# Two FFN layers behind pooled attention: the second layer's table ring in two pools, its first two units interleaved, other store queues

## Chip, cores and metric

The kernel runs on one core of one Trainium2 chip, as one program. The metric is the time of one execution in microseconds on the device; times before are the median of three runs.

## What is computed

The reference, cut to what matters:

```python
# pooled attention: q, k, v are [8, 8, 576, 64]; keys and values are means of 8 positions
k_p = k.reshape(B, H, S // 8, 8, D).mean(axis=3)
v_p = v.reshape(B, H, S // 8, 8, D).mean(axis=3)
x = softmax(scale * q @ k_p.T) @ v_p          # as [4608, 512]
# layer 1: w_in [512, 2048], w_out [2048, 512]
h = x @ w_in
x = (h * clip(h + 3, 0, 6) / 6) @ w_out
# layer 2: w_gate, w_val [512, 1536], w_out [1536, 512]
g = x @ w_gate
out = (g / (1 + exp(-g)) * (x @ w_val)) @ w_out
```

## The kernel before

Every matmul operand in fp32 is split into a rounded part ("hi") and the remainder ("lo"), and a product is hi·hi + hi·lo + lo·hi: three matmuls. Layer 1's down step and all of layer 2 use a seven-product scheme for a 2x2 block product (Strassen in Winograd's form): the quarters 11, 12, 21, 22 of the left operand and sums S1 to S4 of them, those of the right operand and sums T1 to T4, products P1 to P7. The weight side of these sums (the *tables*) is made beside layer 1 and stored in DRAM (`sw1`, `sup`, `sdn`).

The tokens go through layer 1 in nine blocks of 512 (`j`), the up step of all blocks first, then the down step block by block, product by product (`down_b`, `split_b`, `evac_b`; the loop `for i in range(7 * NB)`, n = i mod 7). Its results y go to DRAM by the stores of `evac_b`; in the last block the stores of the products n = 5 and 6 are kept in `last_y` and issued behind the loop, on SyncE's queue, like all the others.

Layer 2 goes through six groups (`p`) of 768 tokens. A group is an up stage of 12 *units* (f, m), where m = 0 is the gate and m = 1 the value table of hidden pair f, and then a down stage of seven products (`down2`, `evac`). A unit is seven products of six matmuls (128x384), each product in a PSUM bank of its own, in the order of the list `UP`: P1 (operand 11), P6 (T2), P5 (T1), P2 (21), P4 (T4), P7 (T3), P3 (22). ScalarE copies P1 out of its bank, VectorE adds the others to that copy (the tiles `c`).

The right operands `xc` of group p + 1 are made from the y of that group (`ystg`) by `x_step` in seven steps: ScalarE casts the hi part, VectorE subtracts for the lo part, and VectorE makes the next sum in place in `ystg`. For group 0 the steps stand at the end of layer 1's last block: step 0 at n = 5, steps 1 to 3 at n = 6, the rest behind the loop. The operand of the last step, T3, is in the pool `xt`, which lies over layer 1's result tiles.

Tables come through a ring of four tiles (`ring`, 8 KB a partition each). A unit takes two: products of the table places 0 to 3 in the first (1024 KB), places 4 to 6 in the second (768 KB). `load_next` issues the next unit's two loads on SyncE's queue. For group 0 it is called at n = 5 and n = 6 of layer 1's last block, then after each unit. The ring's memory is that of layer 1's first weight (`px`) and of operands of its down step (`gq`).

The order on each engine is that of the code (a manual schedule): an instruction that waits holds up all that stands behind it on its engine or queue. Waits between engines are put in from tile uses; with `reuse_waits="tile"` a new tile waits for the last users of the memory it lies over.

Of the kernel before, what the change touches and what calls it, by code (L numbers as in the profile page):

```python
# [23 lines left out]
def kernel(  # L24
# [27 lines left out]
    nc = tc.nc  # L52
# [26 lines left out]
    prep_ctx = ExitStack()  # L79
    s7_p = ctx.enter_context(tc.tile_pool(name="s7", bufs=1, side="right"))  # L80
    q7_p = ctx.enter_context(tc.tile_pool(name="q7", bufs=1, side="right"))
    stg_p = prep_ctx.enter_context(tc.tile_pool(name="stg", bufs=3, side="right"))
# [582 lines left out]
    def x_step(p, n, lo_eng, sum_eng):  # L665
# [10 lines left out]
        xc[p, what] = x  # L676
        split(x[:, 0], x[:, 1], v(what), lo_eng)
        if then:
            sums_b(sum_eng, v, (then,))

    def ring_tile():
        return l2["ring"].tile([P, 2048], F32R, tag="wr", name="wr")
# [65 lines left out]

    TURN = {"11": "11", "22": "22", "21": "12", "12": "21"}
# [28 lines left out]
    def down2(p, n):  # L778
        what = DN[n][0]
        b = dn_b[what] = [bank()[:, :2 * P] for i in range(PT)]  # L780
        for c in range(NPAIR // CH):
            g = gc.pop((p, n, c))
            for t in range(PT):
# [7 lines left out]
    def evac(p, n):  # L791
# [40 lines left out]
        else:  # L832
            add(o_t["o12"], o_t["o12"])
            store("o12", 0, 1)

# [5 lines left out]
    lb, last_y = {}, []  # L841
# [9 lines left out]
    def new_pw(n, t):  # L851
        lb["pw", DN[n][2]] = t.rearrange("p (f a n) -> p f a n", f=NP1, a=2)

    def load_pw(n, half):
        what, fs = DN[n][2], slice(NP1 // 2 * half, NP1 // 2 * (half + 1))
        nc.sync.dma_start(
            out=f32(lb["pw", what][:, fs]).rearrange("p f a n -> p (f a n)"),
# [19 lines left out]
    def down_b(i):  # L877
# [7 lines left out]
        for c in range(NCB):  # L885
            g = gb.pop((i, c))
            for d in range(2):
                for k in range(CB):
                    for m, (wh, gh) in enumerate(((0, 0), (0, 1), (1, 0))):
                        nc.tensor.matmul(  # L890
                            out=ps[:, d], lhsT=w[:, CB * c + k, wh, P * d:P * (d + 1)], rhs=g[:, gh, k],
# [4 lines left out]
    def evac_b(j, n):  # L896
# [11 lines left out]
        def store(tag):  # L908
            r, c = int(tag[1]) - 1, int(tag[2]) - 1
            t0 = N * j + MB * r  # L910
            send = lambda t=ob[tag]: nc.sync.dma_start(out=y_d[:, 2 * c:2 * c + 2, t0:t0 + MB], in_=t)
            if last and n >= 5:
                last_y.append(send)
            else:
                send()
# [227 lines left out]
    with tc.manual_schedule():  # L1143
# [64 lines left out]
        for j in range(NB):  # L1208
            for f in range(F1):
                if (j, f) == (NB - 1, 0):  # L1210
                    attn_ctx.close()
                    for nm in ("px", "gq"):
                        lb[nm] = right_b.enter_context(
# [61 lines left out]
        for send in last_y:  # L1275
            send()
# [64 lines left out]
```

## Time and profile before

| | |
|---|---|
| timed runs, us | 1751.06 median (1749.9 to 1751.83) |
| profiled execution, us | 1746.81 |
| its span, us | 1745.0 |
| TensorE matmul busy, us | 1692.8 (97% of the span) |
| VectorE, ScalarE, GpSimd busy, us | 1334.7, 753.4, 639.0 |
| granted TensorE clock, mean | 0.988 of full speed |
| moved by DMA, MB | 432.47 |

The profiled execution is 4.25 us below the median of the timed runs; sums are made against it. Layer 1's down step ends near 943 us, layer 2 fills the rest. The granted clock has two levels, full (2.4 GHz) and half (1.2 GHz).

### The profile page before, as it was taken

What the parts mean: (1) busy time and instruction counts of PE and PEld (TensorE: products, weight loads), DVE (VectorE), ACT (ScalarE), POOL (GpSimd) and SP (SyncE); (2) the same over time, 40 slices, a digit from 0 to 9 for tenths busy, and PEclk for the clock granted to TensorE, in tenths of its full rate; (3) what the DMA queues carried; (4) which work ended last, traced back from release to release, by engine and by line L of the source; (5) the groups of instructions that cost most, each with busy time, mean ns of one, the idle gap of its engine ahead of it and who ended that gap; (6) DMA issues with size and microseconds to landing.
All of it is one profiled execution on the core that took longest, in us unless ns stands there. A gap on an engine that the chain in (4) does not pass through costs nothing.

```text
span 1745.0 us, 30719 instructions
## 1 busy us (share of the span) xinstructions
PE 1692.8 (97%) x11116; PEld 1598.5 (92%) x11116; DVE 1334.7 (76%) x2356; ACT 753.4 (43%) x1656; POOL 639.0 (37%) x821
## 2 busy tenths in 40 slices
PE   5889999999999999999998999999999999999999
PEld 4678887878788999999998999999999999999999
DVE  6888897788975678888887668668668668668666
ACT  6665555555544455555554224224224224224223
POOL 6554765756821000000000550550550560560560
PEclk8899999999999999999999999999999999999999
DMA  7766898888777965566545878878878878878776
GB/s 184 175 188 176 252 263 242 261 256 256 222 251 278 418 257 174 203 226 216 219 155 188 282 243 289 296 242 291 294 242 292 296 241 289 299 243 285 268 241 218
DMA packets 235832, 432.47 MB, mean 248 GB/s; under 512 B 86688, under 2 KB 168608, under 8 KB 218528
## 3 DMA queue, kind: packets, MB, share of 16 engines
q1 hardware_dynamic: 234624, 430.25, 74.8%
q8 instruction: 88, 1.44, 0.3%
q14 instruction: 64, 0.52, 0.1%
q10 hardware_dynamic: 1056, 0.26, 0.1%
HBM read 326.11 MB, written 104.33 MB: 247 GB/s over the span
## 4 chain that ended last, share of the span: by engine, by line
PE 79%; DVE 8%; DMA 7%; POOL 2%; ACT 2%; issue 1%; SPq 1%; DVEq 0%; POOLq 0%; ACTq 0%
PE b L711 45%; PE b L890 19%; PE h L622 12%; DMA q_in<-in_q_dram 1%; DVE g L637 1%; PE pss L502 1%; DMA qv<-in_q_dram 1%; DMA wstg<-in_moe_w_out_dram 1%; DMA gq<-g 1%; DMA y<-o 1%; DVE mx L512 1%; POOL v_in L441 1%; DMA k_in<-in_k_dram 1%; DVE s L278 1%; DVE qT L484 1%
## 5 line engine op out<-in xcount | busy, mean ns | idle before, releaser
L711 PE MATMUL b<-xc,wr 128*128 128x384 f32 x3024 | 529.1, 336 | 5.2 <-ACT xc L149 2.2
L711 PEld LDWEIGHTS b<-xc,wr 128*128 128x128 f32 x3024 | 526.4, 189 | 6.8 <-ACT xc L149 2.5
L622 PE MATMUL h<-x,wu 128*128 128x512 f32 x1728 | 428.7, 400 | 6.8 <-DVE g L637 6.8
L758 POOL TENSOR_TENSOR s<-s,c 128x384 f32<-128x384 f32 x144 | 142.5, 1014 | 752.3 <-ACT s L756 752.1
L720 DVE TENSOR_TENSOR c<-c,b 128x384 f32<-128x384 f32 x504 | 265.1, 552 | 175.6 <-PE b L711 151.8
L622 PEld LDWEIGHTS h<-x,wu 128*128 128x128 f32 x1728 | 319.3, 190 | 72.2 <-DVE g L637 8.6
L890 PEld LDWEIGHTS b<-gb,pw 128*128 128x128 f32 x3024 | 353.1, 188 | 0.6 <-DVE gb L150 0.5
L890 PE MATMUL b<-gb,pw 128*128 128x256 f32 x3024 | 353.3, 279 | 0.3 <-DVE gb L150 0.3
L711 PE MATMUL b<-wr,gc 128*128 128x256 f32 x2268 | 265.6, 279 | 0.0
L711 PEld LDWEIGHTS b<-wr,gc 128*128 128x128 f32 x2268 | 265.4, 188 | 0.0
L149 ACT CAST gb<-gq 128x512 fp32r<-128x512 f32 x252 | 155.3, 621 | 157.0 <-PE b L890 138.7
L150 DVE TENSOR_TENSOR gb<-gq,gb 128x512 fp32r<-128x512 f32 x252 | 167.4, 689 | 50.7 <-ACT gb L149 50.0
L765 POOL TENSOR_TENSOR gf<-s,c 128x384 f32<-128x384 f32 x144 | 168.2, 1192 | 67.4 <-DVE c L720 64.5
L149 ACT CAST gc<-gf 128x768 fp32r<-128x768 f32 x126 | 105.7, 839 | 187.1 <-POOL gf L765 100.9
L756 ACT ACTIVATE s<-c 128x384 f32<-128x384 f32 x144 | 73.5, 526 | 198.9 <-DVE c L720 197.8
L150 DVE TENSOR_TENSOR gc<-gf,gc 128x768 fp32r<-128x768 f32 x126 | 134.1, 1094 | 16.4 <-ACT gc L149 14.2
L633 ACT ACTIVATE g<-h,half 128x512 f32<-128x512 f32 x144 | 99.0, 687 | 69.7 <-PE h L622 57.5
L637 DVE SCALAR_TENSOR_TENSOR g<-g,h 128x512 f32<-128x512 f32 x144 | 97.4, 677 | 20.2 <-ACT g L633 19.2
L550 POOL TENSOR_TENSOR e<-e,sm 128x288 f32<-128x288 f32 (+4 forms) x74 | 48.1, 650 | 117.7 <-DVE sm L546 95.6
L728 ACT COPY c<-b 128x384 f32<-128x384 f32 x72 | 33.9, 470 | 127.9 <-PE b L711 127.9
L868 DVE TENSOR_TENSOR gq<-gq 128x1024 f32<-128x1024 f32 x72 | 87.8, 1219 | 0.0
L207 DVE TENSOR_TENSOR gf<-gf 128x768 f32<-128x768 f32 (+1 forms) x66 | 67.0, 1030 | 12.2 <-POOL gf L765 10.9
(101 smaller groups left out, 1657.5 us busy)
## 6 DMA issues: line engine op xcount, KB each, us to landing
wr<-sup SPq DMA_DIRECT2D x72, 1024.0 KB
wr<-sdn SPq DMA_DIRECT2D x84, 768.0 KB
wr<-sup SPq DMA_DIRECT2D x72, 768.0 KB
g<-g SPq DMA_DIRECT2D x144, 256.0 KB
gq<-g SPq DMA_DIRECT2D x36, 1024.0 KB
sup<-s SPq DMA_DIRECT2D x12, 1792.0 KB
wstg<-in_moe_w_out_dram SPq DMA_DIRECT2D x56, 256.0 KB
sw<-s SPq DMA_DIRECT2D x8, 1792.0 KB
```

The costliest lines, as they stand in the source:

```text
L149: nc.scalar.copy(out=hi, in_=src)
L150: lo_engine.tensor_tensor(out=lo, in0=src, in1=f32(hi), op=ALU.subtract)
L622: nc.tensor.matmul(out=ps, lhsT=w(kt, wh), rhs=x(kt, xh), start=first and n == 0, stop=last and n == 3 * len(kts) - 1,)
L633: nc.scalar.activation(out=t, in_=ps, func=ACTF.Relu, bias=half, scale=1.0 / 6.0)
L637: nc.vector.scalar_tensor_tensor(out=t, in0=t, scalar=1.0, in1=ps, op0=ALU.min, op1=ALU.mult)
L711: nc.tensor.matmul(out=ps, lhsT=w(wh), rhs=x(xh), start=first and n == 0, stop=last and n == 2)
L720: add = lambda dst, a, b: nc.vector.tensor_tensor(out=dst, in0=a, in1=b, op=ALU.add)
L756: nc.scalar.activation(out=g[q], in_=c[q], func=ACTF.Sigmoid)
L758: nc.gpsimd.tensor_tensor(out=g[q], in0=g[q], in1=c[q], op=ALU.mult)
L765: nc.gpsimd.tensor_tensor(out=gf[p][:, GP[TURN[q]], f], in0=g[q], in1=c[q], op=ALU.mult)
L868: nc.vector.tensor_tensor(out=v(what), in0=v(a), in1=v(b), op=op)
L890: nc.tensor.matmul(out=ps[:, d], lhsT=w[:, CB * c + k, wh, P * d:P * (d + 1)], rhs=g[:, gh, k], start=what == place and (c, d, k, m) == (0 ...
```

## The change

- The ring's four tiles are now two pools of two, `ra` over the memory of layer 1's first weight `pw(0)` (which is now kept in two halves, in tiles of `ra`) and `rb` over operands `gq`. Units take `ra` and `rb` in turn. The first `load_next` stands at n = 2 of layer 1's last block instead of n = 5, the second at n = 5 instead of n = 6.
- The operands T1, 22, T2 are in `xa`; T3, 21, T4 are in `xb`, now on the other side of the memory, over layer 1's weights. The steps go 11, T1, 22, T2, T3, 21, T4.
- The stores of y of the last block are issued on GpSimd's queue, each in its place; `last_y` is gone.
- The first two units of group 0 are made by `up2_pair`, product by product for both m, with P6, P7 and P4 added onto P1's bank and P3 onto P5's.
- In the last group the last down product goes bank by bank, and each third is added and stored by itself.

The core of the diff:

```diff
@@ x_step @@
-        what, then = [("11", "T1"), ("22", "T3"), ("T1", "T2"), ("T2", None), ("21", "T4"), ("T4", None), ("T3", None)][n]
+        what, then = [("11", ("T1",)), ("T1", ()), ("22", ("T3", "T2")), ("T2", ()), ("T3", ()), ("21", ("T4",)), ("T4", ())][n]
         if what == "11":
-            x = new_q7("xc")[:, :4 * M].rearrange("p (a k n) -> p a k n", a=2, k=2)
+            x = new_q7("xc")[:, :4 * M]
+        elif what in ("T1", "22", "T2"):
+            x = l2["xa"].tile([P, 4 * M], F32R, tag="x" + what, name="xc")
         else:
-            pool = l2["xa" if what in ("T1", "22") else "xt" if what == "T3" else "xb"]
-            x = pool.tile([P, 2, 2, M], F32R, tag="x" + what, name="xc")
+            x = l2["xb"].tile([P, 4 * M + 32], F32R, tag="x" + what, name="xc")[:, 8:8 + 4 * M]
...
     def ring_tile():
-        return l2["ring"].tile([P, 2048], F32R, tag="wr", name="wr")
+        n_ring[0] += 1
+        if (n_ring[0] - 1) // 2 % 2:
+            return l2["rb"].tile([P, 2048], F32R, tag="wr", name="wr")
+        return l2["ra"].tile([P, 2048 + 32], F32R, tag="wr", name="wr")[:, :2048]
...
+    def up2_pair(p, f):
+        ps, c, mul = {}, [{}, {}], nc.tensor.matmul
+        for what, wa, xb in [("P1", "11", "11"), ("P5", "S1", "T1"), ("P6", "S2", "T2"), ("P7", "S3", "T3"),
+                             ("P3", "S4", "22"), ("P2", "12", "21"), ("P4", "22", "T4")]:
+            for m in range(2):
+                place = {"P6": "P1", "P7": "P1", "P4": "P1", "P3": "P5"}.get(what, what)
+                if place == what:
+                    ps[m, what] = bank()[:, :M]
+                b, w, x = ps[m, place], wr.pop(("up", (f, m), A7[wa])), xc[p, xb]
+                for n in range(6):
+                    k, (wh, xh) = n // 3, ((0, 0), (0, 1), (1, 0))[n % 3]
+                    mul(out=b, lhsT=w[:, wh, k], rhs=x[:, xh, k], start=place == what and n == 0,
+                        stop=n == 5, skip_group_check=True)
+                new = {"P1": "11", "P6": "12", "P7": "22", "P4": "21"}.get(what)
+                if new:
+                    c[m][new] = tmp(f"c{new}{m}")
+                    nc.scalar.copy(out=c[m][new], in_=b)
+                done = {"P7": ("22", "P5"), "P3": ("12", "P5"), "P2": ("11", "P2")}.get(what)
+                if done:
+                    t = c[m][done[0]]
+                    nc.vector.tensor_tensor(out=t, in0=t, in1=ps[m, done[1]], op=ALU.add)
+        return c
...
@@ down2 @@
+        order = [(c, t) for c in range(NPAIR // CH) for t in range(PT)]
+        if (p, n) == (NG - 1, 6):
+            order.sort(key=lambda ct: ct[1])
@@ evac, last product @@
+        else:
+            o = o_t["o12"]
+            for t in range(PT):
+                nc.vector.tensor_tensor(out=o[:, t], in0=o[:, t], in1=b[t], op=ALU.add)
+                t0 = 2 * M * p + P * t
+                (nc.sync, nc.scalar, nc.sync)[t].dma_start(out=out[t0:t0 + P, 2 * P:], in_=o[:, t])
@@ evac_b @@
-            send = lambda t=ob[tag]: nc.sync.dma_start(out=y_d[:, 2 * c:2 * c + 2, t0:t0 + MB], in_=t)
-            if last and n >= 5:
-                last_y.append(send)
-            else:
-                send()
+            (nc.gpsimd if last else nc.sync).dma_start(out=y_d[:, 2 * c:2 * c + 2, t0:t0 + MB], in_=ob[tag])
@@ layer 1's down loop @@
+            if (j, n) == (NB - 1, 2):
+                load_next()
             if j == NB - 1 and n >= 5:
                 if n == 5:
                     right_b.close()
-                    prep_ctx.close()
-                    for nm, bufs in (("xa", 1), ("ring", 4), ("xb", 1)):
+                    for nm, bufs in (("xa", 1), ("rb", 2)):
...
-                load_next()
+                    load_next()
@@ layer 2 @@
-                c = up2(p, (f, m))
+                if p == f == 0:
+                    if m == 0:
+                        pair = up2_pair(p, f)
+                    c = pair[m]
+                else:
+                    c = up2(p, (f, m))
```

TensorE at the start of layer 2, before: b is the PSUM bank, xc the operand, wr the table tile (11476 and 11478 of the first unit, 11538 and 11540 of the second).

```order
L890 MATMUL b_11489<-gb_11461,pw_7267 128x256 x12
L711 MATMUL b_11587<-xc_11480,wr_11476 128x384 x6
L711 MATMUL b_11596<-xc_11550,wr_11476 128x384 x6
L711 MATMUL b_11605<-xc_11546,wr_11476 128x384 x6
L711 MATMUL b_11614<-xc_11554,wr_11476 128x384 x6
L711 MATMUL b_11622<-xc_11558,wr_11478 128x384 x6
L711 MATMUL b_11630<-xc_11572,wr_11478 128x384 x6
L711 MATMUL b_11640<-xc_11542,wr_11478 128x384 x6
L711 MATMUL b_11664<-xc_11480,wr_11538 128x384 x6
```

The same place now (tables 11271 and 11273 of the first unit, 11476 and 11478 of the second):

```order
L931 MATMUL b_11491<-gb_11466,pw_7268 128x256 x12
L764 MATMUL b_11583<-xc_11480,wr_11271 128x384 x6
L764 MATMUL b_11592<-xc_11480,wr_11476 128x384 x6
L764 MATMUL b_11601<-xc_11540,wr_11271 128x384 x6
L764 MATMUL b_11608<-xc_11540,wr_11476 128x384 x6
L764 MATMUL b_11583<-xc_11548,wr_11271 128x384 x6
L764 MATMUL b_11592<-xc_11548,wr_11476 128x384 x6
L764 MATMUL b_11583<-xc_11561,wr_11273 128x384 x6
L764 MATMUL b_11592<-xc_11561,wr_11478 128x384 x6
```

Each operand now serves two products in a row, one for each unit, and the third pair of products (P6) goes into the banks of the first (11583, 11592).

ScalarE at the same place, before: casts of the operands xc, then the copy of the first P1 (c from bank b) and the sigmoids s.

```order
L149 CAST xc<-ystg 128x768
L927 COPY o_11484<-b 128x512
L149 CAST xc<-ystg 128x768 x6
L728 COPY c_11594<-b 128x384
L756 ACT_TABLE_LOAD
L756 ACTIVATE s_11652<-c_11594 128x384
```

ScalarE now:

```order
L148 CAST xc<-ystg 128x768
L964 COPY o_11484<-b 128x512
L148 CAST xc<-ystg 128x768 x6
L769 COPY c_11590<-b 128x384
L769 COPY c_11599<-b 128x384
L769 COPY c_11621<-b 128x384
L769 COPY c_11629<-b 128x384
L769 COPY c_11637<-b 128x384
L769 COPY c_11646<-b 128x384
```

The six casts stand ahead of the first copy in both; the one copy of a unit has become four, for two units.

SyncE's queue from the load of the first group's y (`ystg`) on, before (sup_107 is the table of unit (0,0), sup_108 of (0,1), sup_109 of (1,0)):

```order
L662 DMA ystg<-y 128x2x384 x4
L690 DMA wr<-sup_107 128x2048
L690 DMA wr<-sup_107 128x1536
L690 DMA wr<-sup_108 128x2048
L690 DMA wr<-sup_108 128x1536
L911 DMA y<-o_11486 128x2x256
L911 DMA y<-o_11484 128x2x256
L911 DMA y<-o_11141 128x2x256
L690 DMA wr<-sup_109 128x2048
```

SyncE's queue now, from the loads of the first table on:

```order
L694 DMA wr<-sup_107 128x2048
L694 DMA wr<-sup_107 128x1536
L661 DMA ystg<-y 128x2x384 x4
L694 DMA wr<-sup_108 128x2048
L694 DMA wr<-sup_108 128x1536
L694 DMA wr<-sup_109 128x2048
L694 DMA wr<-sup_109 128x1536
```

The first table stands ahead of the y loads, and the y stores are gone from this queue.

## Rows read from the trace of the kernel before

**Rows 1.** The page, part 4: the chain's shares of the span by line

```profile
PE b L711 45%; PE b L890 19%; PE h L622 12%; DMA q_in<-in_q_dram 1%; DVE g L637 1%; PE pss L502 1%; DMA qv<-in_q_dram 1%; DMA wstg<-in_moe_w_out_dram 1%; DMA gq<-g 1%; DMA y<-o 1%; DVE mx L512 1%; POOL v_in L441 1%; DMA k_in<-in_k_dram 1%; DVE s L278 1%; DVE qT L484 1%
```

**Rows 2.** The chain in order of time, 900 to 1000 us: start, us, what

```profile
942.00 12.08 DMA y<-o
...
954.10 0.84 ACT xc L149
```

**Rows 3.** TensorE's timeline, 936 to 1090 us: start, us, engine, what, [idle before <-releaser]

```profile
935.77 7.04 PE L890 MATMUL b<-gb,pw 128*128 128x256 f32 x59
944.94 6.38 PE L711 MATMUL b<-xc,wr 128*128 128x384 f32 x25 [2.13 <-DMA wr<-sup]
951.68 1.14 PE L711 MATMUL b<-xc,wr 128*128 128x384 f32 x5 [0.36 <-DVE xc L150]
954.98 0.44 PE L711 MATMUL b<-xc,wr 128*128 128x384 f32 x1 [2.17 <-ACT xc L149]
955.98 83.59 PE L711 MATMUL b<-xc,wr 128*128 128x384 f32 x473 [0.55 <-DVE xc L150]
```

**Rows 4.** Windows: stretch, us, busy time of each engine, PEclk, DMA share, GB/s

```profile
945.00:948.00 3.00, 2.96 (x9) 2.45 (x10) 2.10 (x4) 1.56 (x2) 0.00 (x0) 0.53 1.04 391
...
957.00:959.00 2.00, 2.00 (x8) 2.00 (x8) 1.99 (x5) 0.95 (x2) 0.86 (x1) 0.54 0.01 4
962.00:963.00 1.00, 1.00 (x8) 1.00 (x7) 0.58 (x2) 0.00 (x0) 0.13 (x1) 1.00 0.98 412
963.00:964.00 1.00, 1.00 (x8) 1.00 (x6) 0.51 (x2) 0.00 (x0) 0.00 (x0) 1.00 0.11 43
1006.00:1016.00 10.00, 10.00 (x60) 10.00 (x58) 7.17 (x10) 2.05 (x3) 5.77 (x5) 1.00 0.66 219
```

**Rows 5.** VectorE's timeline, 926 to 956 us, columns as in rows 3

```profile
933.51 1.22 DVE L868 TENSOR_TENSOR gq<-gq 128x1024 f32<-128x1024 f32 x1
...
941.89 0.95 DVE L150 TENSOR_TENSOR xc<-ystg,xc 128x768 fp32r<-128x768 f32 x1
...
944.50 0.95 DVE L212 TENSOR_TENSOR ystg<-ystg 128x768 f32<-128x768 f32 x1
946.35 0.96 DVE L150 TENSOR_TENSOR xc<-ystg,xc 128x768 fp32r<-128x768 f32 x1 [0.90 <-ACT xc L149]
947.22 0.68 DVE L906 TENSOR_TENSOR o<-o,b 128x512 f32<-128x512 f32 x1
947.82 0.95 DVE L150 TENSOR_TENSOR xc<-ystg,xc 128x768 fp32r<-128x768 f32 x1
948.80 0.96 DVE L212 TENSOR_TENSOR ystg<-ystg 128x768 f32<-128x768 f32 x1
```

**Rows 6.** ScalarE's timeline, 935 to 956 us, columns as in rows 3

```profile
945.48 1.56 ACT L149 CAST xc<-ystg 128x768 fp32r<-128x768 f32 x2 [3.95 <-DVE ystg L212]
...
954.84 0.47 ACT L728 COPY c<-b 128x384 f32<-128x384 f32 x1
```

**Rows 7.** SyncE's queue, 936 to 968 us: time of issue, duration of all issues, what

```profile
938.68 2.15 SPq L690 DMA_DIRECT2D wr<-sup  x4
941.28 7.01 SPq L911 DMA_DIRECT2D y<-o  x3
...
959.49 0.33 SPq L690 DMA_DIRECT2D wr<-sup  x1
...
966.79 0.32 SPq L690 DMA_DIRECT2D wr<-sup  x1
```

**Rows 8.** The end: chain, SyncE's queue and windows from 1741 us on

```profile
1741.03 0.42 DVE o L802
...
1741.48 0.37 SPq L810 DMA_DIRECT2D out_dram<-o  x1
...
1742.00:1743.00 1.00, 0.00 (x0) 0.00 (x0) 0.00 (x0) 0.00 (x0) 0.00 (x0) 1.00 0.60 208
1743.00:1744.00 1.00, 0.00 (x0) 0.00 (x0) 0.00 (x0) 0.00 (x0) 0.00 (x0) 0.95 0.54 185
```

More of the change, by code (lines that the diff above doesn't have):

```diff
@@ L78 @@
     ps_a = l1_ps.enter_context(tc.tile_pool(name="ps_a", bufs=2, space=PSUM))
[L79 removed]
     s7_p = ctx.enter_context(tc.tile_pool(name="s7", bufs=1, side="right"))
     q7_p = ctx.enter_context(tc.tile_pool(name="q7", bufs=1, side="right"))
[L82 removed]
+    stg_p = ctx.enter_context(tc.tile_pool(name="stg", bufs=3, side="right"))
     ident = const.tile([P, P], F32, name="ident")
@@ L780, in down2 @@
         b = dn_b[what] = [bank()[:, :2 * P] for i in range(PT)]
-        for c in range(NPAIR // CH):
-            g = gc.pop((p, n, c))
-            for t in range(PT):
+        gs = [gc.pop((p, n, c)) for c in range(NPAIR // CH)]
+        order = [(c, t) for c in range(NPAIR // CH) for t in range(PT)]
+        if (p, n) == (NG - 1, 6):
+            order.sort(key=lambda ct: ct[1])
+        for c, t in order:
+                g = gs[c]
                 for k in range(CH):
@@ L849, in load_g, with new_pw @@
             nc.sync.dma_start(out=t, in_=g_d[j][:, r, c])
-    def new_pw(n, t):
-        lb["pw", DN[n][2]] = t.rearrange("p (f a n) -> p f a n", f=NP1, a=2)
+    HB = BIG // 2
+    def new_pw(n, *halves):
+        if len(halves) == 1:
+            halves = [halves[0][:, HB * h:HB * (h + 1)] for h in range(2)]
+        lb["pw", DN[n][2]] = [t.rearrange("p (f a n) -> p f a n", f=NP1 // 2, a=2) for t in halves]
     def load_pw(n, half):
@@ L856, in load_pw @@
         nc.sync.dma_start(
-            out=f32(lb["pw", what][:, fs]).rearrange("p f a n -> p (f a n)"),
+            out=f32(lb["pw", what][half]).rearrange("p f a n -> p (f a n)"),
             in_=s_w1[:, B7[what], fs].rearrange("p f a n -> p (f a n)"),
@@ L1211 @@
                     attn_ctx.close()
-                    for nm in ("px", "gq"):
-                        lb[nm] = right_b.enter_context(
-                            tc.tile_pool(name=nm, bufs=1, side="right", reuse_waits="tile"))
-                    new_pw(0, lb["px"].tile([P, BIG + 8], F32R, tag="px", name="pw")[:, :BIG])
+                    l2["ra"] = ctx.enter_context(
+                        tc.tile_pool(name="ra", bufs=2, side="right", reuse_waits="tile"))
+                    lb["gq"] = right_b.enter_context(
+                        tc.tile_pool(name="gq", bufs=1, side="right", reuse_waits="tile"))
+                    new_pw(0, *(l2["ra"].tile([P, HB + 32], F32R, tag="wr", name="pw")[:, 24:24 + HB]
+                                for h in range(2)))
                     new_pw(1, big_x("pw"))
@@ L1272 @@
                 load_y(0)
-        for step in (4, 5):
+        left_b.close()
+        l2["xb"] = ctx.enter_context(tc.tile_pool(name="xb", bufs=1, reuse_waits="tile"))
+        for step in (4, 5, 6):
             x_step(0, step, nc.vector, nc.vector)
-        for send in last_y:
-            send()
-        left_b.close()
-        l2["xt"] = ctx.enter_context(tc.tile_pool(name="xt", bufs=1, side="right", reuse_waits="tile"))
-        x_step(0, 6, nc.vector, nc.vector)
         for nm, bufs in (("gf", 1), ("gc", 6), ("t", 1), ("o", 1)):
```

13 lines of the change are left out of this document (7 added, 6 removed).

## Prediction

> **What bounds the kernel now.** I read the page's chain by line first: 45, 19 and 12% of the span are TensorE's products of the three matmul stages, and no other line has more than 1% [rows 1]. So an edit pays only where TensorE stands still, or behind its last matmul. The chain by time shows such a place between layer 1 and layer 2: the chain runs through a 12.08 us store of y and a ScalarE cast that waited for it [rows 2], and is back on TensorE only at 955.98 us. Then TensorE's own timeline of that place. Layer 1's last matmul ends at 935.77 + 7.04 = 942.81 us; layer 2 starts at 944.94, after a wait for its table wr, and stands still again at 951.3, 952.8 and 955.4, for the operands xc [rows 3]. From 955.98 it runs without a gap: 473 recorded matmuls in one row. At full clock 60 of these matmuls go in 10 us, 0.167 us each [rows 4]. A unit of seven products of six matmuls is then 42 x 0.167 = 7.0 us, and the first two units 14.0 us. They end where SyncE gets the last ring tile back, at 966.79 us [rows 7]. So this place loses 966.79 - 942.81 - 14.0 = 10.0 us. That is all there is to win at the boundary, 0.57% of the time.
>
> Why it waits: in the queue of SyncE the loads of the first two units are issued only at 938.68 us, four in a row, and the last three y stores behind them, from 941.28 [rows 7]. The last operand, T3, lies in memory that two of these stores read, hence the 12.08 us in the chain [rows 2].
>
> **The change part by part.** *Early tables, y stores on GpSimd, operands elsewhere.* The tables of unit (0,0) go to two tiles that are free once layer 1's last block is done with its first product's weights, those of (0,1) to two tiles whose last reader is a VectorE sum of that block, over at 933.51 + 1.22 = 934.73 [rows 5], 8 us before layer 2 starts. Even at the slowest load below they land before 942.81, so the wait of 2.13 us for wr goes. T3, 21 and T4 now lie over layer 1 weights that are long read, so no operand waits for a store. The y stores themselves are read four groups later; they cost nothing where they are, if GpSimd's issuing them holds nobody up (a rival, below).
>
> *What is late next.* The pair does each product for both units, in the order 11, T1, T2, T3, 22, 21, T4, and adds P6, P7 and P4 onto P1's bank. So P6 must wait until ScalarE has copied P1 out of that bank. And on ScalarE these copies stand behind all seven operand casts, the last of which, T4, needs nearly the whole operand work of VectorE. I follow that chain with starts from [rows 5]. The first pass after layer 1's adds starts at 941.89, as before. An independent pass follows after 0.87 us (946.35 to 947.22), one that reads what the pass before it wrote after 0.98 (947.82 to 948.80), the pass after a 128x512 add after 0.60 (947.22 to 947.82), and sum, ScalarE cast, low part together take 1.85 (944.50 to 946.35). Low parts of T1 and 22 bring it to 943.63, the sum for T3 to 944.61, sum and cast for T2 to 946.46, its low part to 947.33, the add of o12 to 947.93, the low parts of T3 and 21 to 948.80 and 949.78. There T4's sum starts. Its cast starts 0.98 later, at 950.76 (944.50 to 945.48 in [rows 5, 6]), the copy of P1 0.74 behind that (954.10 to 954.84 in [rows 2, 6]), and takes 0.47: 951.97. Take 952.0.
>
> TensorE meanwhile starts at 942.81 without a wait and has 24 matmuls (P1 and P5 of both units) before P6: 4.0 us, until 946.8. It then stands still for 5.2 us. That is as long as all the pieces of before together (2.13 + 0.36 + 2.17 + 0.55 = 5.2 [rows 3]); but it is one piece.
>
> *The clock.* Before, the granted clock was 0.53 between 945 and 948, after the first idle piece, and 0.54 between 957 and 959, after the later ones [rows 4]. In the first stretch 9 matmuls went in 3 us where 18 would: 9 x 0.167 = 1.5 us. I take one such drop, 1.5 us, where before there were two. Ends: 0.7 us (8 in 2 us where 12 would) and 3.0.
>
> *The rest of the pair.* 60 matmuls are 10.0 us. P3 goes onto P5's bank and has to wait, behind P7, for a copy of 0.47 and an add of at most 0.60 [rows 5, 6] with their hand-offs, against the 1.0 us that the other unit's P7 covers: some 0.4 us (0 to 0.6). The pair ends at 952.0 + 10.0 + 0.4 + 1.5 = 963.9.
>
> *The table of unit (1,0).* Before, each unit gave its tiles back while the other ran. Now both units hold theirs to the end: the first half is read last by P2, and its load is issued when P2 of the first unit is done, 18 matmuls or 3.0 us before the pair's end, at 960.9. How long does 1 MB take? The 768 KB issued at 959.49 were through by 963.8: the DMA share falls from 0.98 to 0.11 [rows 4, 7]. That is 4.3 us; 0.25 MB more at that window's 412 GB/s is 0.6, so I estimate 4.9. With four in flight the first took 944.94 - 938.68 = 6.3. Ends 4.3 and 6.3; nothing else is in flight, so 4.9. It lands at 965.8, and TensorE stands still 1.9 us more. The second half is issued 1.0 us before the pair's end and needed 4.0 us into the unit; it is in time. Then the ring turns as before.
>
> So unit (1,0) starts at 965.8 instead of 966.79: of the 10.0 us that the boundary lost, 5.2 + 1.5 + 0.4 + 1.9 = 9.0 stay. Gain **1.0 us**.
>
> *Last product in three parts.* Before, the last add (0.42) is followed by one store of 384 KB, issued at 1741.48 [rows 8]. Its transfer fills 0.60 + 0.54 = 1.14 us of the DMA windows [rows 8]. Now the first two thirds are done 2.0 and 4.0 us earlier, and 128 KB are left: 0.38 us of transfer. Gain **0.76 us** (0 to 1.14); the latency around it stays. The product's matmuls only change places, and its tables and operands are there.
>
> *At no cost:* the operand steps of later groups in another order (the last, T4, is used after four products or 4.0 us of the next up stage, and behind the last down product come only an add of 0.42 and a pass of 0.95 [rows 5, 8]); the ring in two pools (the same four tiles in turn); layer 1's first weight in two halves. If that cover were gone, each later group would wait about 1 us, five in all.
>
> **The rivals.**
> *B, the waits are shorter.* The clock isn't taken down and the table lands in 4.3 us: 1.5 + 0.4 + 0.6 us less is lost, and the store gives up to 1.14. That is 1.0 + 2.5 + 1.1 = 4.6 us, 1746.5. Against it: the clock fell after both long idle pieces [rows 4], and 5.2 us is longer than either.
> *A, the second wait takes the clock down too,* and the table takes 6.3 us: 1.5 + 1.4 us more is lost, 2.9 against the 1.76 won: 1752.2. For it: the clock fell after 2.13 us [rows 3, 4], and this wait is 1.9 us.
> *C, slower: GpSimd holds up VectorE.* Three y stores are issued by GpSimd just while VectorE runs the chain above. No row shows such an issue; GpSimd did nothing at that place. SyncE's issue of a store is 0.37 us [rows 8], and that is the low end. From 1.7 us for each of the three on, it costs over 1.7 + 3.5 us and decides; with 2 us each it is 6 us, 1755.3. Against it: between 1006 and 1016 GpSimd is busy 5.77 us beside VectorE's 7.17, and TensorE waits for neither [rows 4]. The Trainium skill (SBUF — State Buffer, "Who interferes with whom") says that a GpSimd DMA's descriptors are written by GpSimd itself through a port shared with VectorE, that copies in VectorE's fast modes lock it, but that tensor_tensor takes only the read side, which descriptor writing does not need. By that rule the chain, all TENSOR_TENSOR passes [rows 5], is not held and C costs nothing; no run here shows it yet. The same section advises the SP or ACT queue, against this change.
> *The change doesn't do what it says:* the tables of unit (0,1) could still be late. That would be a wait after the first product; but it would come out of the 5.2 us, as the P1 copy is what P6 waits for.
>
> **How the numbers follow.** The profiled execution took 1746.81 us, a span of 1745.0 and 1.8 around it. 1.0 + 0.76 = 1.76 us less give 1745.05 there. The median of the three timed runs is 1751.06, 4.25 above; the same sum gives 1749.3. Chances: forecast 0.60, A 0.20, B 0.14, C 0.06. About 0.2%, 3.5 us, is what a measurement of this kernel can tell from no change: the forecast (1749.3) and A (1752.2) lie within, B (1746.5) is faster, C slower. So faster 0.14, same 0.80, slower 0.06. The range leaves out C and the outer half of B: 1747.0 to 1753.0.
>
> **What would show it.** Right: no TensorE wait for wr or a y store at the first product; one idle piece of about 5 us after 24 matmuls, ended by ScalarE's copy of P1; granted clock about half in a stretch behind it; a second piece of about 2 us after 84 matmuls, ended by a wr load; steady from there; a last store of 128 KB, and some 0.8 us less behind the last matmul. Wrong: P6 starting right at 946.8 (then up to 9 us are won), VectorE's passes stretched while GpSimd issues, or waits of TensorE in later up stages.

## Result, and the profile of the changed kernel

The changed kernel takes 1759.07 us (median of four runs, 1758.57 to 1759.26), the kernel before 1750.48 us beside it (four runs, 1747.89 to 1751.83). The ratio is 1.0051, 95% interval 1.0035 to 1.0067: half a per cent slower. The forecast was 1749.3 (1747.0 to 1753.0) with 0.06 for slower, so it was wrong in sign and in range. The prediction worked from the median of the first three runs before, 1751.06.

The profiled execution of the changed kernel took 1759.26 us, with a span of 1757.1; before it was 1746.81 and 1745.0. TensorE's timeline between layer 1 and layer 2 answers to [rows 3]. The columns are start, us, engine, line, what, and in brackets the idle time before and what ended it; neighbouring rows overlap a little, because a matmul's modelled end lies behind the next one's start. So a stage's length, from its start to the next stage's start, is about 0.16 us less than the duration in its row; where two stages are compared, both are taken the same way.

```profile
935.83 8.68 PE L931 MATMUL b<-gb,pw 128*128 128x256 f32 x73
944.35 4.33 PE L764 MATMUL b<-xc,wr 128*128 128x384 f32 x24
953.75 13.70 PE L764 MATMUL b<-xc,wr 128*128 128x384 f32 x60 [5.07 <-ACT c L769]
969.62 75.06 PE L715 MATMUL b<-xc,wr 128*128 128x384 f32 x420 [2.17 <-DMA wr<-sup]
1044.52 45.08 PE L715 MATMUL b<-wr,gc 128*128 128x256 f32 x378
1089.43 88.04 PE L715 MATMUL b<-xc,wr 128*128 128x384 f32 x504
1177.31 45.13 PE L715 MATMUL b<-wr,gc 128*128 128x256 f32 x378
```

Down to the fourth row the shape is the one that was forecast: no wait for a table at the first product, 24 matmuls, one idle piece of 5.07 us ended by ScalarE's copy of P1, 60 matmuls, one piece of 2.17 us ended by a ring load. From there TensorE never waits. But look at the steady stages. The same stages of the kernel before, from its timeline:

```profile
1039.40 44.26 PE L711 MATMUL b<-wr,gc 128*128 128x256 f32 x378
1083.50 87.53 PE L711 MATMUL b<-xc,wr 128*128 128x384 f32 x504
```

A down stage of 378 matmuls was 1083.50 - 1039.40 = 44.10 us long and is now 1089.43 - 1044.52 = 44.91; an up stage of 504 matmuls was 87.37 and is now 1177.31 - 1089.43 = 87.88. No row shows an idle piece in either. Each matmul comes a little later behind the one before it: 44.10 us over 378 matmuls, 116.7 ns each, became 118.8, and 87.37 over 504, 173.4, became 174.4. The page's groups say the same where one knows to look: the down group's mean went from 279 to 281 ns and its busy time from 265.6 to 270.6 us. The granted clock is 1.00 in both of these stages, so the clock is not the reason. That is a busy TensorE that does the same work more slowly.

The chain of waits at the boundary (start, us, what):

```profile
952.49 0.83 ACT xc L148
953.32 0.39 ACT c L769
953.75 5.95 PE b L764 x18
...
964.33 5.25 DMA wr<-sup
```

The granted clock there, in windows (stretch, us, busy time of PE, PEld, DVE, ACT, POOL, then PEclk, DMA share, GB/s):

```profile
953.00:959.00 6.00, 5.25 (x16) 5.25 (x17) 0.96 (x1) 2.03 (x5) 0.00 (x0) 0.50 0.00 0
...
970.00:973.00 3.00, 3.00 (x11) 3.00 (x11) 0.00 (x0) 1.52 (x4) 3.00 (x4) 0.51 0.95 372
973.00:976.00 3.00, 3.00 (x19) 3.00 (x18) 1.45 (x3) 0.00 (x0) 3.00 (x4) 1.00 0.88 366
```

Half clock, 1.2 GHz, twice: behind the first idle piece and again behind the second.

The end answers to [rows 8]: the last matmul ends at 1753.74, the last add follows at once, and the span ends 3.4 us behind that matmul; before it was 1745.0 - 1741.01 = 4.0.

```profile
1753.77 0.42 DVE o L868
```

Where the 12.1 us between the two spans lie, stage start by stage start:

| stretch | before | after | difference, us |
|---|---|---|---|
| start to layer 1's down step | 589.21 | 590.78 | +1.6 |
| layer 1's down step | 353.6 | 353.7 | +0.1 |
| its last matmul to unit (1,0) | 966.79 - 942.81 = 24.0 | 969.62 - 944.51 = 25.1 | +1.1 |
| rest of the first up stage | 72.6 | 74.9 | +2.3 |
| five later up stages | 87.37 each | 87.88 each | +2.6 |
| six down stages | 44.10 each | 44.94 each (mean) | +5.0 |
| behind the last matmul | 4.0 | 3.4 | -0.6 |

Here 966.79 is the release that the prediction took for the unit's start. The first line is put down to the run and not to the change: the instructions of that stretch stand in the same order, and in the twelve profiles of this study, of kernels that share that stretch, it ends between 588.2 and 598.2. The timed medians are only 8.6 us apart because before's profiled execution lay 3.7 us below its median, and the changed kernel's at it. So below, kernels are compared from layer 1's last matmul to their last matmul: 798.2 us before (942.81 to 1741.01), 809.2 after.

### The profile page after: what moved, and what is told of

It reads as the page before. It is cut to its first block, busy times and chain, and to the rows that moved or that the text cites. A ratio compares the mean times of both kernels' runs of the same rounds, so it can differ in the third digit from the quotient of the medians.

```text
span 1757.1 us, 30694 instructions
## 1 busy us (share of the span) xinstructions
PE 1704.8 (97%) x11116; PEld 1610.3 (92%) x11116; DVE 1332.9 (76%) x2348; ACT 755.8 (43%) x1662; POOL 643.9 (37%) x825
## 4 chain that ended last, share of the span: by engine, by line
PE 81%; DVE 9%; DMA 5%; ACT 2%; issue 1%; POOL 1%; SPq 1%; DVEq 0%; ACTq 0%; POOLq 0%
PE b L715 45%; PE b L931 19%; PE h L621 14%; DMA q_in<-in_q_dram 1%; DVE g L636 1%; PE pss L501 1%; DMA qv<-in_q_dram 1%; DVE s L277 1%; DVE mx L511 1%; DMA gq<-g 1%; DVE qT L483 1%; DVE q L140 1%; PE b L764 1%; DVE x L614 0%; DMA g<-g 0%
## 5 line engine op out<-in xcount | busy, mean ns | idle before, releaser
L715 PE MATMUL b<-xc,wr 128*128 128x384 f32 x2940 | 515.3, 336 | 2.2 <-DMA wr<-sup 2.2
L715 PEld LDWEIGHTS b<-xc,wr 128*128 128x128 f32 x2940 | 513.9, 188 | 2.5 <-DMA wr<-sup 2.5
L724 DVE TENSOR_TENSOR c<-c,b 128x384 f32<-128x384 f32 x490 | 258.4, 552 | 180.0 <-PE b L715 141.3
L931 PE MATMUL b<-gb,pw 128*128 128x256 f32 x3024 | 353.7, 279 | 0.1
L715 PE MATMUL b<-wr,gc 128*128 128x256 f32 x2268 | 270.6, 281 | 0.0
L715 PEld LDWEIGHTS b<-wr,gc 128*128 128x128 f32 x2268 | 270.4, 190 | 0.0
L636 DVE SCALAR_TENSOR_TENSOR g<-g,h 128x512 f32<-128x512 f32 x144 | 97.4, 677 | 20.5 <-ACT g L632 19.4
```

Source lines behind the costliest of these rows:

```text
L636: nc.vector.scalar_tensor_tensor(out=t, in0=t, scalar=1.0, in1=ps, op0=ALU.min, op1=ALU.mult)
L715: nc.tensor.matmul(out=ps, lhsT=w(wh), rhs=x(xh), start=first and n == 0, stop=last and n == 2)
L724: add = lambda dst, a, b: nc.vector.tensor_tensor(out=dst, in0=a, in1=b, op=ALU.add)
L931: nc.tensor.matmul(out=ps[:, d], lhsT=w[h][:, fh, wh, P * d:P * (d + 1)], rhs=g[:, gh, k], start=what == place and (c, d, k, m) == (0, 0, ...
```

## Experiments

**Is the slower pace the place of the tiles, or the traffic beside them?** The change pads tiles: `ra` tiles and the operands in `xb` are 32 numbers (128 bytes) longer than their data. So the tiles of a set, which before lay at equal distances modulo 256 bytes from the tiles that they are multiplied with, no longer do. "Distance" below is the byte address in SBUF of the moving operand minus that of the stationary one, modulo 256, from the addresses that the kernel's tiles were allocated, which are not in the profile. Before, all up products have distance 0 and all down products 32. After, 1080 of 3024 up products have 128, and 1701 of 2268 down products 160. The first run pads by 64 numbers, 256 bytes, instead, which brings every product back to 0 or 32, and keeps all else:

```diff
-            x = l2["xb"].tile([P, 4 * M + 32], F32R, tag="x" + what, name="xc")[:, 8:8 + 4 * M]
+            x = l2["xb"].tile([P, 4 * M + 64], F32R, tag="x" + what, name="xc")[:, 8:8 + 4 * M]
...
-        return l2["ra"].tile([P, 2048 + 32], F32R, tag="wr", name="wr")[:, :2048]
+        return l2["ra"].tile([P, 2048 + 64], F32R, tag="wr", name="wr")[:, :2048]
...
-                    new_pw(0, *(l2["ra"].tile([P, HB + 32], F32R, tag="wr", name="pw")[:, 24:24 + HB]
+                    new_pw(0, *(l2["ra"].tile([P, HB + 64], F32R, tag="wr", name="pw")[:, 56:56 + HB]
```

> The changed kernel with its tiles padded so that the byte addresses of the two operands of every matmul of the down steps and of layer 2 differ by the same amount modulo 256 as in the kernel before (0 in the up stages, 32 in the down stages; in the changed kernel 1080 of 3024 up matmuls have 128 and 1701 of 2268 down matmuls have 160). Theory place: that difference sets the matmuls' pace, so one group of layer 2 takes 87.4 + 44.1 us again instead of 87.9 + 44.9, 8 us less in six groups: about 1751 us. Theory traffic (something else in the changed kernel, like stores on GpSimd's queue or other neighbours in memory, slows the matmuls): stays at 87.9 + 44.9 and 1759 us. Both: the wait at the start of layer 2 stays, one piece of 5 us ended by ScalarE's copy and one of 2 us ended by a wr load.

1752.7 us (median of 10 runs), ratio to before 1.001 (0.9993 to 1.0027). Its TensorE timeline:

```profile
929.77 12.18 PE L931 MATMUL b<-gb,pw 128*128 128x256 f32 x103
941.79 4.33 PE L764 MATMUL b<-xc,wr 128*128 128x384 f32 x24
951.19 12.57 PE L764 MATMUL b<-xc,wr 128*128 128x384 f32 x60 [5.08 <-ACT c L769]
966.02 73.09 PE L715 MATMUL b<-xc,wr 128*128 128x384 f32 x420 [2.26 <-DMA wr<-sup]
1038.96 44.26 PE L715 MATMUL b<-wr,gc 128*128 128x256 f32 x378
1083.06 87.53 PE L715 MATMUL b<-xc,wr 128*128 128x384 f32 x504
```

The steady stages are those of before to a hundredth: 44.26 and 87.53 us. Everything else of the change is still in, GpSimd's queue and the two pools too. So the place of the tiles is the cause of the slower pace, and the other traffic is not. The boundary is what it was: 966.02 - 941.95 = 24.1 us, the two idle pieces are still there, and from layer 1's last matmul to the last one it is 798.6 us. With the distances of before, the change comes out at nothing.

**The same from the other side.** The kernel before, with only the down operands `gc` moved by 128 bytes (a pad of 32 numbers on the tile below them), so that every down product has distance 160:

```diff
-            gf[p] = l2["gf"].tile([P, 4, NPAIR, M], F32, tag="gf", name="gf")
+            gf[p] = l2["gf"].tile([P, 4 * NPAIR * M + 32], F32, tag="gf", name="gf")[:, :4 * NPAIR * M].rearrange(
+                "p (s f n) -> p s f n", s=4, f=NPAIR)
```

> The kernel before, with one pad of 128 bytes ahead of the operand tiles gc, so that the difference modulo 256 of all 2268 down matmuls of layer 2 is 160 instead of 32; nothing else is changed. Place: down stages of 45.2 us instead of 44.1 (378 x 119.7 ns instead of 116.7), up stages unchanged at 87.4: 6.8 us slower, about 1757 us. Traffic: no change, 1750.5 us.

1753.06 us (10 runs), ratio to before 1.001 (0.9994 to 1.0026). Two stages of its timeline:

```profile
1048.63 44.52 PE L711 MATMUL b<-wr,gc 128*128 128x256 f32 x378
1092.98 87.53 PE L711 MATMUL b<-xc,wr 128*128 128x384 f32 x504
```

Only the down stage changes, as it should, but by 0.26 us (44.52 against 44.26) and not by the 1.1 that was expected: 117.3 ns a matmul. The direction holds; the size doesn't, though the distance is that of the changed kernel. Six times 0.26 is 1.6 us, too little for the timed runs to tell.

**A table of distances.** Two kernels shift the operands of the kernel before by another amount in each of the six groups (`SHIFT`, in numbers of 4 bytes; the tiles get 64 numbers of room). The first:

```diff
+    SHIFT = (0, 8, 16, 24, 32, 48)
...
-            x = pool.tile([P, 2, 2, M], F32R, tag="x" + what, name="xc")
+            x = pool.tile([P, 4 * M + 64], F32R, tag="x" + what, name="xc")
+        x = x[:, SHIFT[p]:SHIFT[p] + 4 * M].rearrange("p (a k n) -> p a k n", a=2, k=2)
...
-        t = gc[p, n, c] = l2["gc"].tile([P, 2, CH, M], F32R, tag="gc", name="gc")
+        g0 = SHIFT[p]
+        t = l2["gc"].tile([P, 2 * CH * M + 64], F32R, tag="gc", name="gc")[:, g0:g0 + 2 * CH * M]
```

> The kernel before with the operands xc and gc of group 0 to 5 shifted by 0, 32, 64, 96, 128 and 192 bytes. One look at the trace: place expects up stages of 87.4 us where the difference is 0 and 88.7 (176 ns a matmul) at 128, down stages of 44.1 at 32 and 45.2 at 160, and tells what lies between: a step at 128, if only that bit counts, or a slope. Traffic: all six groups alike.

1754.99 us, one run. Some of its stages from the second group on, one up and one down row to a group. The six groups' up stages lie at 0, 32, 64, 96, 128 and 192. In a down stage the shifted tile `gc` is the stationary operand, so the same shifts give 32, 0, 224, 192, 160 and 96 there:

```profile
1083.29 87.52 PE L713 MATMUL b<-xc,wr 128*128 128x384 f32 x504
1170.65 45.51 PE L713 MATMUL b<-wr,gc 128*128 128x256 f32 x378
...
1348.10 89.20 PE L713 MATMUL b<-xc,wr 128*128 128x384 f32 x504
1437.13 44.68 PE L713 MATMUL b<-wr,gc 128*128 128x256 f32 x378
1481.65 88.87 PE L713 MATMUL b<-xc,wr 128*128 128x384 f32 x504
```

The second takes other shifts, with a list of its own for the down operands:

```diff
+    SHIFT = (4, 12, 2, 56, 40, 60)
+    GSHIFT = (56, 40, 4, 60, 2, 62)
...
+        g0 = GSHIFT[p]
```

> The kernel before with other distances in each of the six groups: up stages at 16, 48, 8, 224, 160 and 240 bytes modulo 256 (groups 0 to 5), down stages at 64, 128, 16, 48, 24 and 40. Theory (the pace follows the distance; up 0 to 64 as in the kernel before, 96 to 192 slower by 2.6 to 3.3 ns; down fastest near 32): up 16, 48 and 8 give 87.53 us, 224 and 240 between 87.5 and 89.2, 160 about 89; down 16 to 48 about 44.26, 64 and 128 up to 45.5. None is expected to be faster than the kernel before; one that is would be the distance to take. Rival (only multiples of 32 or 64 matter): 8, 16, 24, 40 and 48 fall together with 0, 32 or 64.

1755.35 us, one run. Its up stages lie at 16, 48, 8, 224, 160 and 240, its down stages at 64, 128, 16, 48, 24 and 40; the rows at up 160, up 240 and down 40:

```profile
1481.33 87.53 PE L714 MATMUL b<-xc,wr 128*128 128x384 f32 x504
...
1613.42 90.84 PE L714 MATMUL b<-xc,wr 128*128 128x384 f32 x504
1704.10 45.52 PE L714 MATMUL b<-wr,gc 128*128 128x256 f32 x378
```

Stage times of both, with up 0 from the kernel before, in us as the timelines' rows show them:

| distance | 0 | 8 | 16 | 32 | 48 | 64 | 96 | 128 | 160 | 192 | 224 | 240 |
|---|---|---|---|---|---|---|---|---|---|---|---|---|
| up stage | 87.53 | 87.52 | 88.7 (est.) | 87.52 | 88.36 | 87.53 | 89.20 | 88.87 | 87.53 | 89.20 | 87.54 | 90.84 |

| distance | 0 | 16 | 24 | 32 | 40 | 48 | 64 | 96 | 128 | 160 | 192 | 224 |
|---|---|---|---|---|---|---|---|---|---|---|---|---|
| down stage | 45.51 | 44.51 | 44.90 | 44.26 | 45.52 | 44.27 | 44.69 | 45.52 | 45.03 | 44.52 | 44.68 | 44.89 |

(Up at 16 fell into the first group, whose stage holds the boundary; 88.7 is worked out from 175.6 ns between its matmuls' starts.) Up spreads by 3.3 us a stage, down by 1.26. The expectation for the second was of a smooth curve, and it fell: up at 160 is as fast as at 0, up at 240 the slowest of all, down at 40 much slower than at 32 and 48. The rival's multiples of 32 or 64 do not fit either. No distance was faster than those of the kernel before. The granted clock is 1.00 in the slowest of these stages too.

**Why 160 costs 117.3 ns in one kernel and 119.6 in another.** The starts of single matmuls at distance 160 show two patterns. Where every tile lies at 160 (the run with `gc` moved) five intervals repeat to within 1 ns, from 115 to 120 ns, mean 117.3. In the changed kernel most run at 119, 120, 121, mean 119.6, and behind the products of the one tile at 32 shorter ones mix in for a while. The next run therefore gives the kernel before the mixture of the changed one: `gc` moved as above, and one ring tile of four moved too.

```diff
...
+        n_ring[0] += 1
+        o = 32 * (n_ring[0] % 4 == 0)
-        return l2["ring"].tile([P, 2048], F32R, tag="wr", name="wr")
+        return l2["ring"].tile([P, 2048 + 64], F32R, tag="wr", name="wr")[:, o:o + 2048]
```

> The kernel before with its down operands shifted by 128 bytes (distance 160 to every ring tile), and with the fourth of the four ring tiles shifted by 128 bytes too, so that three ring tiles lie at 160 and one at 32, as in the changed kernel; in the up stages every fourth tile then lies at 128 instead of 0. Theory (at 160 the pace has two patterns, and a tile at another distance in between throws it from the one that gave 117.3 ns when all tiles lay at 160 into that of 119 to 120): down stages 44.9 us as in the changed kernel, up stages 87.8. Rival (the changed kernel's slower pace at 160 comes from something else in it, such as which engine writes at that time): 44.4 us, 117.3 ns at 160 and 116.7 at 32.

1755.56 us, one run. One down and one up stage:

```profile
1041.80 45.13 PE L715 MATMUL b<-wr,gc 128*128 128x256 f32 x378
1086.76 87.81 PE L715 MATMUL b<-xc,wr 128*128 128x384 f32 x504
```

45.13 us is the changed kernel's down stage (45.08 to 45.13), now without any of its instructions moved; at 160 the intervals are 119.6 ns, at 32 116.9. So the mixture of distances makes the loss, and a tile's pace depends on the tiles beside it as well as on its own distance. That speaks for the distance and not for the address of one operand: at 32, both operands of this run lie 128 bytes off those of before (modulo 256), where a matmul took 116.7. In the other direction, the changed kernel with only the `xb` pad at 64 numbers, which leaves 648 up products at 128 and 567 down products at 160:

```diff
-            x = l2["xb"].tile([P, 4 * M + 32], F32R, tag="x" + what, name="xc")[:, 8:8 + 4 * M]
+            x = l2["xb"].tile([P, 4 * M + 64], F32R, tag="x" + what, name="xc")[:, 8:8 + 4 * M]
```

> The changed kernel with one pad changed: the operand tiles of T3, 21 and T4 are 64 instead of 32 numbers longer than their data, so that all three lie at the same distance modulo 256 bytes from each other; the ring's two tiles ra keep their pad of 32, so that one of the four ring tiles differs from the others by 128. Theory (pace follows the byte distance of the two operands modulo 256): distance 128 is left for 648 of 3024 products of a pass through the six up stages instead of 1080, and the down stages have three ring tiles at 32 (116.7 ns) and one at 160 instead of one and three. Up stages 87.75 us (87.88 in the changed kernel, 87.53 with none), down stages 44.4 to 44.5 (44.93, 44.26). Rival (the pace follows something else that came with the change): 87.88 and 44.93 stay.

1756.2 us, one run.

```profile
1046.08 44.54 PE L715 MATMUL b<-wr,gc 128*128 128x256 f32 x378
1090.46 87.82 PE L715 MATMUL b<-xc,wr 128*128 128x384 f32 x504
```

Both stages lie between the two kernels, near the expected 44.4 to 44.5 and 87.75. (That expectation mixes the two ways to take a stage; from start to start they are 44.38 and 87.64 to 87.66.)

**The tail alone.** The kernel before with nothing but the last product bank by bank and stored in three parts (the order of its matmuls, cut here, is that of the change):

```diff
...
-        else:
+        elif p < NG - 1:
             add(o_t["o12"], o_t["o12"])
             store("o12", 0, 1)
+        else:
+            o = o_t["o12"]
+            for t in range(PT):
+                nc.vector.tensor_tensor(out=o[:, t], in0=o[:, t], in1=b[t], op=ALU.add)
+                t0 = 2 * M * p + P * t
+                (nc.sync, nc.scalar, nc.sync)[t].dma_start(out=out[t0:t0 + P, 2 * P:], in_=o[:, t])
```

> The kernel before with the last product alone changed: bank by bank, stored in three parts. From the last matmul to the end of the span 3.4 us as in the changed kernel instead of 4.0; a time some 0.6 us lower, which one run can't show. If the last 128 KB cost as much as 384 KB: 4.0.

1747.98 us, one run. Its last matmul ends at 1743.25 of a span of 1746.3: 3.05 us, against 4.0 before and 3.4 expected. The transfer that is left is short in the windows (share of the DMA engines 0.38 in one of the three microseconds, where [rows 8] show 0.60 and 0.54):

```profile
1744.00:1745.00 1.00, 0.00 (x0) 0.00 (x0) 0.00 (x0) 0.00 (x0) 0.00 (x0) 1.00 0.38 129
```

**Can the boundary's gain be had?** The next three start from the run with pads of 64. The first moves the T4 step (its cast, low part) behind P6's copies, and P2 ahead of P3, so that the first half of the ring comes free earlier:

```diff
-                             ("P3", "S4", "22"), ("P2", "12", "21"), ("P4", "22", "T4")]:
+                             ("P2", "12", "21"), ("P3", "S4", "22"), ("P4", "22", "T4")]:
+            if what == "P7":
+                x_step(p, 6, nc.vector, nc.vector)
...
-        for step in (4, 5, 6):
+        for step in (4, 5):
```

> The changed kernel with the operand and table tiles back at the distances of the kernel before, and with two moves at the boundary: the cast and low part of T4 are emitted behind P6's copies, and the pair's products go P1, P5, P6, P7, P2, P3, P4. Theory (the boundary loses what P1's copy behind the T4 cast and the late first half of the ring cost): read from the run with mended distances, P1's copy follows the third cast at 947.0 instead of 950.7 us, so P6 waits 1.3 instead of 5.1 us; P2's first unit ends 5 us before the pair does, so the table of unit (1,0) lands in time and the second wait of 2.3 us is gone, and with the long wait the half-clock spell. Unit (1,0) starts 16 us behind layer 1's last matmul (15.8 to 17.5), against 24.1; down stages 44.26, up stages 87.53 us. Time 8 us below the run with mended distances (6 to 8.3), ratio to before about 0.996. Rival (the waits of this place only move: T4, P3's bank or the second half of the ring is late next): 19 us or more, ratio 0.998 or above.

1741.02 us (5 runs, 1739.77 to 1745.4), ratio to before 0.9954 (0.9938 to 0.997): 0.46% below the kernel before, and below the changed kernel.

```profile
933.75 10.42 PE L933 MATMUL b<-gb,pw 128*128 128x256 f32 x88
944.01 4.33 PE L766 MATMUL b<-xc,wr 128*128 128x384 f32 x24
949.69 10.70 PE L766 MATMUL b<-xc,wr 128*128 128x384 f32 x60 [1.35 <-ACT c L771]
960.40 73.10 PE L715 MATMUL b<-xc,wr 128*128 128x384 f32 x420
```

960.40 - 944.17 = 16.2 us, against 24.1. One idle piece of 1.35 us is left, and ScalarE's timeline shows why it is short: the P1 copies follow three casts at once, and the T4 cast comes later, in front of P7's copies.

```profile
946.97 2.30 ACT L148 CAST xc<-ystg 128x768 fp32r<-128x768 f32 x3 [3.35 <-DVE ystg L211]
949.17 0.85 ACT L771 COPY c<-b 128x384 f32<-128x384 f32 x2
...
952.48 0.84 ACT L148 CAST xc<-ystg 128x768 fp32r<-128x768 f32 x1
```

The ring's load is hidden, and the windows from 940 to 964 show the granted clock at 1.00 throughout. From layer 1's last matmul to the last one it is 1734.94 - 944.17 = 790.8 us, 7.4 below before and 7.8 below the run with pads of 64.

The second moves T4 alone and keeps the order P7, P3, P2, P4:

> As the run before it, but with the pair's products in the changed kernel's order (P7, P3, P2, P4): only the T4 cast is moved. Theory: P6 waits 1.3 us, P3 0.8 (VectorE's low part of T4 stands ahead of the add that frees its bank), and the table of unit (1,0), loaded once P2 of the first unit is done, still makes TensorE wait some 1.9 us. Unit (1,0) starts 18.5 us (17.5 to 20.5) behind layer 1's last matmul; 5.5 us below the run with mended distances (3.5 to 6.5). Rival as above: 22 us or more.

1747.55 us (10 runs), ratio 0.9986 (0.9974 to 0.9998).

```profile
954.98 4.46 PE L766 MATMUL b<-xc,wr 128*128 128x384 f32 x24 [1.27 <-ACT c L771]
960.12 6.52 PE L766 MATMUL b<-xc,wr 128*128 128x384 f32 x36 [0.68 <-DVE c L775]
968.79 74.67 PE L715 MATMUL b<-xc,wr 128*128 128x384 f32 x420 [2.16 <-DMA wr<-sup]
```

Layer 1's last matmul ended at 949.51, so unit (1,0) starts 19.3 us behind it (18.5 expected, 17.5 to 20.5): the long piece is gone, P3's wait is 0.68, and the ring load is late as before. The clock is down behind that last wait (0.69 between 968 and 972), so the first up stage takes 1.6 us more than above. P2's place decides over that.

The third drops the pair:

```diff
-                if p == f == 0:
-                    if m == 0:
-                        pair = up2_pair(p, f)
-                    c = pair[m]
-                else:
-                    c = up2(p, (f, m))
+                c = up2(p, (f, m))
```

> The changed kernel with the distances of the kernel before, and without the pair: the first two units run one after the other as in the kernel before, with the early tables and the y stores on GpSimd's queue kept. Theory: no wait for a table at the first product; the second product waits for T2's low part (3.6 us), the fifth for T4's (1.8 us), nothing after that, and one spell of half clock costs 1.5 to 3 us: unit (1,0) starts 21.5 to 23.5 us behind layer 1's last matmul, 1 to 2.5 us better than with the pair (24.1). Rival (the pair is worth its two waits): 25 us or more.

1748.45 us, one run.

```profile
948.55 1.21 PE L715 MATMUL b<-xc,wr 128*128 128x384 f32 x6
952.38 0.44 PE L715 MATMUL b<-xc,wr 128*128 128x384 f32 x1 [2.62 <-ACT xc L148]
953.37 4.96 PE L715 MATMUL b<-xc,wr 128*128 128x384 f32 x18 [0.55 <-DVE xc L149]
958.55 83.33 PE L715 MATMUL b<-xc,wr 128*128 128x384 f32 x479 [0.23 <-DVE xc L149]
```

No wait for a table; three shorter ones for operands, 3.4 us together where 5.4 was expected. The down stage starts at 1041.72; 72.9 us of up stage less, unit (1,0) starts at 968.8, 20.1 us behind layer 1's last matmul at 948.7 (21.5 to 23.5 expected). So without the pair 4.0 us of the 24.1 are saved, and the pair as written loses them again.

That it takes the change's early tables to earn those 4.0 us is not shown: the kernel before gets nearly as much when its tiles lie elsewhere. In the first of the two kernels with shifted operands, whose instructions are those of before and whose first group has the distances of before, layer 1's last matmul ends at 945.85, and then:

```profile
945.69 1.21 PE L713 MATMUL b<-xc,wr 128*128 128x384 f32 x6
...
1039.19 44.26 PE L713 MATMUL b<-wr,gc 128*128 128x256 f32 x378
```

There is no wait for a table here and none for a y store, and the first down stage starts 93.3 us behind that matmul: 96.6 in the kernel before, 93.0 without the pair. Its longer operand tiles move the ring, so that by the kernel's allocation its first tile lies over another operand `gq`, and the first load is issued 8.1 us ahead of that matmul's end (4.1 before):

```profile
937.72 4.73 SPq L692 DMA_DIRECT2D wr<-sup  x4
```

## Why the prediction was wrong

**The step that failed is one clause of "At no cost": the ring in two pools, "the same four tiles in turn".** They are not at the same addresses, and neither are the operands. The pads of 128 bytes stood in the diff, and the prediction has no term for them: it put what lies where at nothing. The two steady lines of the table above, 2.6 + 5.0 us, and about 0.4 of the first up stage come to 8.0 us, and the run with pads of 64 took that pace away. That alone carries the forecast of 1749.3 to 1757.3, out of its range; the timed medians lie 8.6 us apart. Nothing in the trace of before could show it, since there all tiles of a set have one distance; that was a reason to put a bound on it, and there was none. The signs of being wrong that the prediction lists (P6 without a wait, stretched passes of VectorE, waits in later up stages) did not come; a slower pace without a wait is not among them.

**The clock was mis-sized.** The prediction took one drop of 1.5 us, ends 0.7 and 3.0. The first drop cost 13.70 - 10.70 = 3.0 us, by the same 60 matmuls in the run with P2 moved; in the two runs with the changed kernel's boundary and other pads (64 everywhere, and 64 on `xb` alone), behind the same wait of 5.08 us, they took 12.57 and 12.58, so it cost 1.9. The second, rival A's, came too: the first up stage was 1044.52 - 969.62 = 74.9 us, 2.0 more than with pads of 64 (72.9), of which 0.4 is pace; some 1.5 us stay. So 4.5 us in place of 1.5 in this profile. In those two other runs the second wait, 2.26 and 2.20 us, was not followed by half clock, and the whole came to 1.9. So 2.6 of the 4.5 us are not shown to belong to the change.

**The rest of the boundary held.** First idle piece 5.2 forecast, 5.07 measured, ended by the copy behind the T4 cast. The table's transfer 4.9 forecast, 5.25 measured; the wait for it 1.9 forecast, 2.17 measured. P3's wait, 0.4 forecast, can't be seen. The unit of 42 matmuls was taken at 7.0 us from [rows 4]; 42 x 0.1734 is 7.3, so the boundary lost some 9.4 us before instead of 10.0, and the same error is in the pair's 60 matmuls, 10.4 instead of 10.0. Taken together the boundary came out 1.1 us longer, where 1.0 us shorter was forecast. One profile of it is not worth more than 2 us: the run with only the tail changed has before's boundary, and its last matmul ends 796.5 us behind layer 1's instead of 798.2.

**The tail:** 0.76 forecast, 0.6 measured here, and 0.95 alone.

**Rival C, GpSimd holding VectorE up, didn't happen.** GpSimd issued two y stores at 943.26 us, in 1.46 us, and VectorE's passes around them took what [rows 5] give: two independent 128x768 passes 0.87 + 0.95 = 1.82, two sums, the later one reading the earlier, 0.98 + 0.96 = 1.94.

```profile
943.26 1.46 POOL L952 DMA_DIRECT2D y<-o  x2 [17.98 <-DVE o L947]
...
942.26 1.40 DVE L947 TENSOR_TENSOR o<-o,b 128x512 f32<-128x512 f32 x2
943.59 1.82 DVE L149 TENSOR_TENSOR xc<-ystg,xc 128x768 fp32r<-128x768 f32 x2
945.32 1.95 DVE L211 TENSOR_TENSOR ystg<-ystg 128x768 f32<-128x768 f32 x2
```

The third store was issued at 950.03, and the two independent passes beside it took 1.82 as well. The trace agrees here with the Trainium skill (SBUF — State Buffer, "Who interferes with whom"), by which such passes are not held. The slower side of the forecast hung on this rival alone; the loss came from a place that had no rival.

The same section of the Trainium skill, on that page, lists two read ports for TensorE, one for the moving operand and one for the weight load, and calls them independent. From that alone one would not expect the place of the two operands to matter to the pace. The kernel before with nothing but tiles moved (`gc`; `gc` and one ring tile of four) went from 44.10 to 44.35 and 44.96 us a down stage; the measurement decides. Whether those two reads are what meets is not shown by these runs.

## What to carry to other kernels

Where a change moves or pads tiles that TensorE reads, work out the byte addresses of moving against stationary operand before and after, and keep them: a busy engine without an idle row can still be slower, and the start-to-start time of its matmuls in a steady stage is the number to look at. When an accumulation saves banks by going onto one that must be copied first, that copy's place in the queue of its engine belongs to the change; here one cast moved behind it and one product moved forward turned nothing into 0.46%. When a tile changes its length, look also at what the tiles behind it now lie over: a first load can go out earlier or later by that alone. Compare runs from a mark behind the parts that the change doesn't touch.

## What was not expected of the hardware

- **Matmul pace follows where the operands lie.** For 128x384 matmuls of this kernel an up stage took 87.52 to 90.84 us, for 128x256 a down stage 44.26 to 45.52, by tile addresses alone, at full clock and without a wait. It is no smooth function of the distance modulo 256 (up: 160 as fast as 0, 240 the slowest), and at one distance there are two patterns, 117.3 and 119.6 ns at 160, of which the mixture of tiles around decides. The rule behind it stays open.
- **The same idle time does not always take the clock down.** Waits of 2.17 us (the changed kernel, granted clock 0.51 behind it) and 2.16 us (T4 moved alone, 0.69) did; 2.26 us (pads of 64, clock 1.00 from 966 to 970) and 2.20 us (64 on `xb` alone, 1.00 from 973 to 976) did not, nor did 1.35 us. Each of the first two cost 1.5 to 1.6 us. The wait of some 5.1 us took the clock down in all three runs that have it, for 3.0, 1.9 and 1.9 us. A forecast should give a wait of about 2 us both outcomes.
